# Router logits of chunks 0 to 7 on VectorE, with the rows of chunks 0 to 6 read back from DRAM

## The chip, the cores and the metric

One core of a Trainium2 chip runs the whole program. The metric is the device time of one execution in microseconds. A few words are used throughout: PE is TensorE's matrix multiply, PEld its weight load, DVE is VectorE, ACT is ScalarE, POOL is GpSimd, SP the engine that issues most DMAs. L1083 is line 1083 of the kernel before; the changed kernel has other line numbers, which are given where they matter.

## The reference

```python
def _attn_ref(q, k, v):                 # 4 batches, 8 heads, 576 positions, 64 dims
    ...
    return (out_up + out_local)         # pooled attention plus a band of +-3 positions
def _moe_ref(x, w_gate, w_val, w_out):  # x: 2304 tokens x 512
    g = x @ w_gate                      # 512 x 1536
    silu = g * (1.0 / (1.0 + np.exp(-g)))
    return silu * (x @ w_val) @ w_out   # 1536 x 512
def _moe2_ref(x, expert_emb, tau, w1, w2):
    xn = x / (np.linalg.norm(x, axis=-1, keepdims=True) + 1e-06)
    en = expert_emb / (np.linalg.norm(expert_emb, axis=-1, keepdims=True) + 1e-06)
    logits = xn @ en.T / tau            # 8 experts
    expert_idx = np.argmax(logits, axis=1)
    ...
    for e in range(E):                  # each token goes to one expert
        h = np.maximum(x[mask] @ w1[e], 0.0)
        out[mask] = gate_w[mask, None] * (h @ w2[e])
```

The three run one after another: attention, a gated layer, and a layer of eight experts of which each token uses one. The router needs, for each token, its norm and its eight logits.

## The kernel before, in words

The 2304 tokens are cut into nine chunks of 256 (`NCHUNK` is 9, `CT` is 256), numbered 0 to 8. A chunk's rows come in two blocks `m` of 128 tokens. Every fp32 product is made of three fast ones, with each operand split into a high and a low part.

For a chunk, `gemm1(c, p)` computes one of six blocks `p` of the hidden layer (L982); each has two **halves** `j`, of 24 matmuls, and one PSUM bank per half. `act_h` then works on a half: ACT tanh (L931), two DVE operations (L933, L935), an ACT cast (L938), and a subtraction on DVE or POOL (L940) that gives the low part. `gemm2(c, p)` multiplies that block by `w_out` (L1014) in four groups of three matmuls, and accumulates x2, the layer's output, in two PSUM banks. Chunks 0 and 1 run interleaved block by block; from chunk 2 on the order is one chunk after another. `gemm2` of a block comes one block later than its `gemm1`, and the last two blocks' second products stand together before the next chunk's first.

`x_split` and `x_piece` cut the attention's output of a chunk into high and low parts (L918 on ACT, L920 on DVE or POOL). There is one pair of buffers for it, so that a chunk's pieces are made after the last `gemm1` of the chunk before.

When x2 of a chunk is complete, `route(c)` is started. `route_m` copies each block of 128 rows to SBUF (L1051), has `store_x2` write it to the DRAM tensor `x2d` (L1205), and takes the sum of squares (L1054). Then the logits are made in one of two ways, by `ROWS_C`:

- Chunks 0 to 4 and 8: four transposes on PE (L1063), a copy to SBUF (L1068), and four matmuls with the normalised expert embeddings (L1073).
- Chunks 5 to 7: `route_rows`, eight DVE operations per block of rows (L1083). Each multiplies the 128x512 rows by one embedding, which lies on all partitions, and sums along the row. The embeddings are loaded for that by `prep_rows`, once attention has freed its buffers.

After that `route` scales the logits, takes the maximum and its index (L1127 to L1134), counts with two small matmuls on PE (L1143, L1144) at which place in its expert's list each token stands, and has POOL scatter the token numbers into the DRAM table `tab` (L1162, two indirect DMAs). Each chunk's `route` waits for the table entries of the chunk before, since `base`, the running count, goes from one to the next.

Expert 0's first two blocks of 128 places are filled from chunks 0 to 7 alone. `load_slots` reads the table, `load_slot` gathers the x2 rows by an indirect DMA on POOL (L1299), PE transposes them (L1309), ACT and DVE split them, and `expert(0)` begins (L1353) while chunk 8 is still being routed. `load_experts` and `split_w` load 64 pieces of expert weights and split them on ACT (L1238) and DVE (L1241).

The order on each engine is fixed at build time by a list scheduler, `Sched`: every operation has a cost in ns and a priority (a lower number goes first), and the scheduler walks through simulated time and gives each free engine the ready operation of the lowest number. `how=True` marks DVE operations that it doesn't let overlap with POOL's. On the chip each engine runs its list in order and waits by semaphores. Three lines of the part that the change touches:

```python
yield op("DVE", t_dve(DM) + 60, -0.3, True)                       # L1082, logits on DVE
yield op(("DVE", "POOL"), (t_dve(n), pool(n)), prio, True)        # both(): L920, L940
yield op("DVE", t_dve(CT), -0.5)                                  # L932, activation
```

Of the kernel before, what the change touches and what calls it, by code (L numbers as in the profile page):

```python
# [24 lines left out]
P = 128  # L25
B, H, S, D = 4, 8, 576, 64
HP = H // 2
DM = H * D
# [220 lines left out]
EARLY_N = range(NE)  # L249
ROWS_C = range(5, NCHUNK - 1)  # L250
NV = 4
# [6 lines left out]
def build(tc, a):  # L258
# [221 lines left out]

    en_rows = []

    def prep_rows():

        for n in range(B * HP):
            yield ("wait", ("done", n))
        sl = []
        for _ in range(5):
            sl.append((yield ("get", "aw")))
        for i in range(E // 2):  # L490
            yield dma(P * 4096)
            nc.sync.dma_start(out=sl[i], in_=bass.AP(tensor=end.tensor, offset=end.offset + 2 * i * DM, ap=[[0, P], [1, 2 * DM]]))
            en_rows.extend((sl[i][:, 0:DM], sl[i][:, DM:2 * DM]))
        en_rows.extend((sl[4][:, 0:DM], sl[4][:, DM:2 * DM]))
        sc.set("rows")

    def pget(n=1):
# [416 lines left out]
    def x_piece(c, k, xh, xl):  # L914
        yield ("wait", ("xr", c, k))
        src = x32[c][:, k, :]
        yield op("ACT", t_act(256), -1.0)
        nc.scalar.copy(xh[:, k, :], src)  # L918
        e = yield both(CT, -1.0)
        on[e].tensor_tensor(out=xl[:, k, :], in0=src, in1=xh[:, k, :], op=ALU.subtract)  # L920
        sc.set(("x", c, k))
# [71 lines left out]
    def gemm2(c, p):  # L993
# [3 lines left out]
        if p == NFB - 1:  # L997
            sc.spawn((c + 1) * 10 - 1, route(c))
        yield ("wait", ("w_out", p))
# [44 lines left out]
    def route_m(c, m, sv, lp):  # L1044
# [11 lines left out]
        if c in ROWS_C:  # L1056
            sc.put(x2cls(c), xp)
            sc.spawn(sc.cur.prio, route_rows(c, m, row, lp))
            return
# [5 lines left out]
        tcls = "w" if c == NCHUNK - 1 else "t2"  # L1065
        x2T = last_T[m] if last_T else (yield ("get", tcls))
        eng = yield psum(DM, hi)
# [10 lines left out]
    def route_rows(c, m, row, lp):  # L1078

        yield ("wait", "rows")  # L1080
        for e in range(E):
            yield op("DVE", t_dve(DM) + 60, -0.3, True)  # L1082
            nc.vector.scalar_tensor_tensor(out=en_rows[E + m], in0=row, scalar=1.0, in1=en_rows[e], op0=ALU.mult, op1=ALU.mult,  # L1083
                                           accum_out=lp[:, m, e:e + 1])
        sc.set(("rowT", c, m))
        sc.set(("lg", c, m))

    def route_norm(c, m, sv):
# [7 lines left out]
        sc.set(("norm", c, m))  # L1096

    last_T = []

    def route(c):  # L1100
        hi = -1.0
        if c == NCHUNK - 1:
            for m in range(2):
                last_T.append((yield ("get", "w")))
        if c > 0:
# [3 lines left out]
        lg, oh, t8, mx, mxi = lgt  # L1109
        sv = gm.tile([P, 4, 2], F32, tag="sv", name=f"sv{c}")  # L1110
        si = gm.tile([P, 2], I32, tag="si", name=f"si{c}")
        yield ("wait", ("x2", c, 0))
        if c in ROWS_C:
            lgs = lr = gm.tile([P, 2, E], F32, tag="lr", name=f"lr{c}")
        else:
            lp = lr = yield ("get", "ps")
            lgs = lp[:, 0:2 * E].rearrange("p (m e) -> p m e", m=2)
        for m in range(2):
            if c == NCHUNK - 1:
                sc.spawn(sc.cur.prio, route_m(c, m, sv, lr))  # L1120
            else:
                yield from route_m(c, m, sv, lr)
        for m in range(2):
# [105 lines left out]
    def stand_back():  # L1229

        if ("x2", NCHUNK - 1, 0) in sc.ev:
            yield ("wait", ("slot", NCHUNK - 1))
# [305 lines left out]
    with tc.manual_schedule():  # L1538
# [9 lines left out]
        sc.spawn(3, prep_en(), 0.0)  # L1548
        sc.spawn(3, prep_rows(), 0.0)
        for c in range(NCHUNK):  # L1550
            if c != 1:
# [126 lines left out]
```

## Time and profile before

| | |
|---|---|
| Runs | 867.78, 868.7, 866.0 us (median 867.78) |
| The profiled execution | 868.81 us, of which its span is 866.6 us |
| PE busy | 849.0 us, 98% of the span |
| DVE busy | 504.9 us, 58% |
| ACT busy | 377.1 us, 44% |
| POOL busy | 154.9 us, 18% |
| Mean granted clock of TensorE | 0.992 |

The profile is of one execution. Its span runs from the first to the last instruction that was recorded; 2.2 us of its own time lie outside. It can be read by stage: attention with the first chunks (to about 395 us), chunks 4 to 8 of the gated layer, the experts from 590 us, and the last scatters after 857 us.

### The profile page before, as it was taken

The page shows a single profiled execution, that of the slowest core. Times are in us where ns is not written, and L with a number is a line of the kernel's source. Part 1 is how long each engine was busy: PE and PEld are TensorE (multiplying, and loading weights), DVE is VectorE, ACT ScalarE, POOL GpSimd, SP SyncE. Part 2 cuts the span into 40 slices and gives each one's busy share as a digit, 9 for nine tenths or more (in the row PEclk, how much of TensorE's full clock was granted, in tenths as well). Part 3 has the DMA queues.
Part 4 walks back from the last instruction along what each step waited for, and adds up shares of the span by engine and source line. Part 5 has one row for each costly group of instructions (what it writes and reads, how often), then busy time and mean ns, then how long its engine had stood idle before and what let it go on. Part 6 is the DMA issues. An engine that isn't in the chain of part 4 may idle for free. (4 is left out here: it accounts for less than half of the span.)

```text
span 866.6 us, 17180 instructions
## 1 busy us (share of the span) xinstructions
PE 849.0 (98%) x6904; PEld 759.1 (88%) x6905; DVE 504.9 (58%) x1230; ACT 377.1 (44%) x906; POOL 154.9 (18%) x163
## 2 busy tenths in 40 slices
PE   9999999999999999999999999999999999999995
PEld 4788889999989989999999999999988888888884
DVE  4899999566555365673373654967464544545210
ACT  3878789444343243342221313345354444445120
POOL 4552300022102011010000000021310330331111
PEclk9999999999999999999999999999999999999998
DMA  8593445112121002122000000464565554453100
GB/s 255 191 327 119 137 155 178 54 37 83 57 82 58 1 26 58 57 83 98 2 25 1 25 1 26 123 194 122 153 206 177 169 182 148 161 186 120 30 27 28
DMA packets 53219, 90.21 MB, mean 104 GB/s; under 512 B 7878, under 2 KB 24646, under 8 KB 53136
## 3 DMA queue, kind: packets, MB, share of 16 engines
q1 hardware_dynamic: 48256, 78.83, 28.7%
q0 software_dynamic: 4160, 9.48, 3.3%
q8 instruction: 55, 0.90, 0.4%
q10 hardware_dynamic: 720, 0.77, 0.3%
q14 instruction: 28, 0.23, 0.1%
HBM read 80.05 MB, written 10.58 MB: 105 GB/s over the span
## 5 line engine op out<-in xcount | busy, mean ns | idle before, releaser
L982 PE MATMUL ps<-xhi,w 128*128 128x256 f32 x1504 | 294.0, 288 | 1.7 <-POOL w L428 1.3
L982 PEld LDWEIGHTS ps<-xhi,w 128*128 128x128 f32 x1504 | 242.5, 192 | 5.3 <-POOL w L428 1.5
L982 PE MATMUL ps<-xlo,w 128*128 128x256 f32 x752 | 213.3, 284 | 0.0
L982 PEld LDWEIGHTS ps<-xlo,w 128*128 128x128 f32 x752 | 144.7, 192 | 1.4
L1353 PE MATMUL ps<-xh,w 128*128 128x336 f32 (+1 forms) x512 | 124.3, 315 | 0.0
L1014 PE MATMUL x<-w,hh 128*128 128x512 f32 x384 | 120.9, 396 | 0.0
L933 DVE SCALAR_TENSOR_TENSOR th<-th,ps 128x256 f32<-128x256 f32 x108 | 45.1, 418 | 108.4 <-ACT th L931 106.0
L931 ACT ACTIVATE th<-ps 128x256 f32<-128x256 f32 x108 | 41.0, 380 | 128.5 <-PE ps L982 128.0
L1353 PEld LDWEIGHTS ps<-xh,w 128*128 128x128 f32 x512 | 88.3, 188 | 2.3
L1241 DVE TENSOR_TENSOR w<-w,w 128x1024 fp32r<-128x1024 f32 x64 | 76.9, 1217 | 21.8 <-ACT w L1238 20.9
L1353 PE MATMUL ps<-xl,w 128*128 128x336 f32 (+1 forms) x256 | 79.9, 312 | 0.0
L1014 PEld LDWEIGHTS x<-w,hh 128*128 128x128 f32 x384 | 68.3, 189 | 12.1 <-issue 0.4
L938 ACT CAST hh<-th 128x256 fp32r<-128x256 f32 x108 | 43.7, 405 | 79.9 <-DVE th L935 79.3
L1363 PE MATMUL x<-w,eh 128*128 128x512 f32 x248 | 78.3, 397 | 0.0
L1339 DVE SCALAR_TENSOR_TENSOR el<-ps,eh 128x336 fp32r<-128x336 f32 (+1 forms) x62 | 30.3, 493 | 80.6 <-ACT eh L1337 80.4
L1014 PE MATMUL x<-w,hl 128*128 128x512 f32 x192 | 74.9, 390 | 0.0
L1337 ACT ACTIVATE eh<-ps 128x336 fp32r<-128x336 f32 (+1 forms) x62 | 27.5, 443 | 90.7 <-PE ps L1353 84.6
L1238 ACT CAST w<-w 128x1024 fp32r<-128x1024 f32 x64 | 65.6, 1044 | 0.0
L1091 POOL TENSOR_TENSOR sv<-sv,half 128x1 f32<-128x1 f32 x18 | 10.4, 580 | 250.6 <-ACT x L1054 244.9
L1378 POOL DMA_INDIRECT out<-sg,tb x23 | 23.2, 1007 | 174.7 <-ACT sg L1370 166.1
L940 DVE TENSOR_TENSOR hl<-th,hh 128x256 fp32r<-128x256 f32 x94 | 39.8, 424 | 24.7 <-ACT hh L938 24.6
L1363 PEld LDWEIGHTS x<-w,eh 128*128 128x128 f32 x248 | 45.2, 188 | 9.0
(262 smaller groups left out, 1403.5 us busy)
## 6 DMA issues: line engine op xcount, KB each, us to landing
w<-w SPq DMA_DIRECT2D x64, 512.0 KB
w<-w_gate SPq DMA_DIRECT2D x10, 512.0 KB
w<-w_val SPq DMA_DIRECT2D x10, 512.0 KB
w<-w_out SPq DMA_DIRECT2D x10, 512.0 KB
w<-qk SPq DMA_DIRECT2D x16, 291.0 KB
aw<-qk SPq DMA_DIRECT2D x16, 291.0 KB
x2d<-sg SPq DMA_DIRECT2D x18, 256.0 KB
w<-vw SPq DMA_DIRECT2D x8, 320.0 KB
```

Of the source, the lines that this page charges most:

```text
L931: nc.scalar.activation(th, ps[:, 0:CT], AF.Tanh, scale=0.5)
L933: nc.vector.scalar_tensor_tensor(out=th, in0=th, scalar=1.0, in1=ps[:, 0:CT], op0=ALU.add, op1=ALU.mult)
L938: nc.scalar.copy(hh[:, j].bitcast(F32R), th)
L940: on[e].tensor_tensor(out=hl[:, j].bitcast(F32R), in0=th, in1=hh[:, j].bitcast(F32R), op=ALU.subtract)
L982: nc.tensor.matmul(ps[:, o:o + CT], ww[:, k, fs], xx[:, k, :], start=(k == 0 and n == 0), stop=(k == KD - 1 and n == 2))
L1014: nc.tensor.matmul(x2p[c, m], l[:, j, ms], r[:, js], start=(p == 0 and j == 0 and n == 0), stop=(p == NFB - 1 and j == 1 and n == 2))
L1238: nc.scalar.copy(hi.bitcast(F32R), raw)
L1241: nc.vector.tensor_tensor(out=lo.bitcast(F32R), in0=raw, in1=hi.bitcast(F32R), op=ALU.subtract)
L1337: nc.scalar.activation(hh[:, j, 0:n].bitcast(F32R), ps[:, 0:n], AF.Relu)
L1339: nc.vector.scalar_tensor_tensor(out=hl[:, j, 0:n].bitcast(F32R), in0=ps[:, 0:n], scalar=0.0, in1=hh[:, j, 0:n].bitcast(F32R), op0=ALU.max ...
L1353: nc.tensor.matmul(ps[:, 0:n], ww[:, k, fs], xx[:, k, 0:n], start=(k == 0 and t == 0), stop=(k == KD - 1 and t == 2))
L1363: nc.tensor.matmul(yt[:m], l, r, start=(first and n == 0), stop=(last and n == 2))
```

## The change

Logits of chunks 0 to 7 are all made on DVE. `ROWS_C` goes from chunks 5 to 7 to chunks 0 to 7, and the new `LATER` names chunks 0 to 6. For a chunk of `ROWS_C`, `gemm2` now starts `keep_rows`, which copies the rows, stores them to `x2d` and takes the norms; `route(c)` is started at the beginning of the program and waits for the norms and the logits. For a chunk of `LATER` the row buffer is free after the store, and `route_rows` waits until the embeddings are there (`rows`), takes one of three buffers `again` (half of an `aw` buffer and two halves of an `x32` buffer), reads the block of 128 rows back from `x2d` by a DMA on SP, and runs the eight multiplications. All of these write their product to the same scratch row `en_rows[E]`, where there were two, and their cost in the scheduler is 50 ns less.

Besides: pieces of x of chunks 3 to 8 go from priority -1.0 to -0.4, behind the activations' -0.5. `stand_back`, which holds the splits of expert weights back for the routing of chunk 8, does so from the last block of chunk 8 on. The two buffers for chunk 8's transposed rows are taken before the expert weights' (`last_slots`).

```diff
 EARLY_N = range(NE)
-ROWS_C = range(5, NCHUNK - 1)
+LATER = range(0, NCHUNK - 2)
+ROWS_C = range(0, NCHUNK - 1)
 NV = 4
...
-    en_rows = []
+    en_rows, again, svs, lrs = [], [], {}, {}
...
-        en_rows.extend((sl[4][:, 0:DM], sl[4][:, DM:2 * DM]))
+        en_rows.append(sl[4][:, 0:DM])
+        again.append(sl[4][:, DM:2 * DM])
+        sc.put("again", 0)
         sc.set("rows")
+        x = yield ("get", "x32")
+        x = x.rearrange("p k n -> p (k n)")
+        for i in range(2):
+            again.append(x[:, i * DM:(i + 1) * DM])
+            sc.put("again", i + 1)
...
     def x_piece(c, k, xh, xl):
         yield ("wait", ("xr", c, k))
         src = x32[c][:, k, :]
-        yield op("ACT", t_act(256), -1.0)
+        hi = -1.0 if c < 3 else -0.4
+        yield op("ACT", t_act(256), hi)
         nc.scalar.copy(xh[:, k, :], src)
-        e = yield both(CT, -1.0)
+        e = yield both(CT, hi)
         on[e].tensor_tensor(out=xl[:, k, :], in0=src, in1=xh[:, k, :], op=ALU.subtract)
...
         if p == NFB - 1:
-            sc.spawn((c + 1) * 10 - 1, route(c))
+            sc.spawn((c + 1) * 10 - 1, keep_rows(c) if c in ROWS_C else route(c))
...
         if c in ROWS_C:
             sc.put(x2cls(c), xp)
+            if c in LATER:
+                sc.set(("rowT", c, m))
             sc.spawn(sc.cur.prio, route_rows(c, m, row, lp))
             return
...
         sc.set(("rowT", c, m))
         tcls = "w" if c == NCHUNK - 1 else "t2"
-        x2T = last_T[m] if last_T else (yield ("get", tcls))
+        x2T = last_T[m] if c == NCHUNK - 1 else (yield ("get", "t2"))
         eng = yield psum(DM, hi)
         copy[eng](x2T[:, 0:DM], xp)
         sc.put(x2cls(c), xp)
...
         yield ("wait", "rows")
+        if c in LATER:
+            yield ("wait", ("x2d", c, m))
+            i = yield ("get", "again")
+            row = again[i]
+            yield dma(P * 2048)
+            t = 2 * c + m
+            nc.sync.dma_start(out=row, in_=x2d[t * P:(t + 1) * P, :])
         for e in range(E):
-            yield op("DVE", t_dve(DM) + 60, -0.3, True)
-            nc.vector.scalar_tensor_tensor(out=en_rows[E + m], in0=row, scalar=1.0, in1=en_rows[e], op0=ALU.mult, op1=ALU.mult,
+            yield op("DVE", t_dve(DM) + 10, -0.3, True)
+            nc.vector.scalar_tensor_tensor(out=en_rows[E], in0=row, scalar=1.0, in1=en_rows[e], op0=ALU.mult, op1=ALU.mult,
                                            accum_out=lp[:, m, e:e + 1])
-        sc.set(("rowT", c, m))
+        if c in LATER:
+            sc.put("again", i)
+        else:
+            sc.set(("rowT", c, m))
         sc.set(("lg", c, m))
...
+    def norms(c):
+        svs[c] = gm.tile([P, 4, 2], F32, tag=f"sv{c % 7}", name=f"sv{c}")
+        return svs[c]
+
+    def keep_rows(c):
+        sv = norms(c)
+        lrs[c] = gm.tile([P, 2, E], F32, tag=f"lr{c % 6}", name=f"lr{c}")
+        for m in range(2):
+            yield from route_m(c, m, sv, lrs[c])
+
     last_T = []
+
+    def last_slots():
+        yield ("wait", ("g1", NCHUNK - 2))
+        for m in range(2):
+            last_T.append((yield ("get", "w")))
...
     def route(c):
         hi = -1.0
-        if c == NCHUNK - 1:
+        if c in ROWS_C:
             for m in range(2):
-                last_T.append((yield ("get", "w")))
+                yield ("wait", ("norm", c, m))
+                yield ("wait", ("lg", c, m))
         if c > 0:
             yield ("wait", ("tab", c - 1))
         lgt = [gm.tile([P, 2, E], t, tag=nm, name=f"{nm}{c}") for nm, t in
                (("lg", F32), ("oh", F32R), ("t8", F32), ("mx", F32), ("mxi", U32))]
         lg, oh, t8, mx, mxi = lgt
-        sv = gm.tile([P, 4, 2], F32, tag="sv", name=f"sv{c}")
+        sv = svs[c] if c in ROWS_C else norms(c)
         si = gm.tile([P, 2], I32, tag="si", name=f"si{c}")
         yield ("wait", ("x2", c, 0))
         if c in ROWS_C:
-            lgs = lr = gm.tile([P, 2, E], F32, tag="lr", name=f"lr{c}")
+            lgs = lrs[c]
         else:
-            lp = lr = yield ("get", "ps")
+            lp = yield ("get", "ps")
             lgs = lp[:, 0:2 * E].rearrange("p (m e) -> p m e", m=2)
-        for m in range(2):
-            if c == NCHUNK - 1:
-                sc.spawn(sc.cur.prio, route_m(c, m, sv, lr))
-            else:
-                yield from route_m(c, m, sv, lr)
+            for m in range(2):
+                if c == NCHUNK - 1:
+                    sc.spawn(sc.cur.prio, route_m(c, m, sv, lp))
+                else:
+                    yield from route_m(c, m, sv, lp)
...
     def stand_back():
 
-        if ("x2", NCHUNK - 1, 0) in sc.ev:
+        if ("h", NCHUNK - 1, NFB - 1, 0) in sc.ev:
             yield ("wait", ("slot", NCHUNK - 1))
...
+        sc.spawn(NCHUNK * 10 + 3, last_slots(), 0.0)
+        for c in ROWS_C:
+            sc.spawn((c + 1) * 10 - 1, route(c), 0.0)
```

The built order shows what moves. First PE, in the second products (L1014, in the changed kernel L1023) around the routing of chunk 1, `x` being the x2 banks and `sg` the rows. Before:

```order
L1014 MATMUL x_1_112<-w_1_629,hl_1_99 128x512
L1063 MATMUL ps_1_106<-cn,sg_1_103 128x128 x4
L1014 MATMUL x_1_111<-w_1_629,hh_1_97 128x512
L1014 MATMUL x_1_111<-w_1_630,hh_1_97 128x512
L1014 MATMUL x_1_111<-w_1_629,hl_1_99 128x512
L1014 MATMUL x_1_112<-w_1_629,hh_1_97 128x512
L1014 MATMUL x_1_112<-w_1_630,hh_1_97 128x512
L1014 MATMUL x_1_112<-w_1_629,hl_1_99 128x512
L1073 MATMUL ps_1_108<-enT,sg_1_104 128x8 x4
L1014 MATMUL x_1_111<-w_1_629,hh_1_97 128x512
L1014 MATMUL x_1_111<-w_1_630,hh_1_97 128x512
L1014 MATMUL x_1_111<-w_1_629,hl_1_99 128x512
```

Now:

```order
L1023 MATMUL x_1_112<-w_1_629,hl_1_99 128x512
L862 MATMUL ps_1_108<-aw_3_2174 64x144 x4
L871 MATMUL ps_1_105<-aw_3_2175 64x58 x8
L871 MATMUL ps_1_105<-aw_2_2313,aw_3_2175 64x58 x8
L871 MATMUL ps_1_108<-aw_3_2175 64x58 x2
L871 MATMUL ps_1_108<-aw_3_2175 64x54 x2
L1023 MATMUL x_1_111<-w_1_629,hh_1_97 128x512
L1023 MATMUL x_1_111<-w_1_630,hh_1_97 128x512
L1023 MATMUL x_1_111<-w_1_629,hl_1_99 128x512
L1023 MATMUL x_1_112<-w_1_629,hh_1_97 128x512
L1023 MATMUL x_1_112<-w_1_630,hh_1_97 128x512
L1023 MATMUL x_1_112<-w_1_629,hl_1_99 128x512
```

The four transposes (L1063) and the four matmuls with the embeddings (L1073) are gone; part of an attention head (L862, L871) stands there instead, which had another place before.

Next DVE in the middle of chunk 6, three halves' activations (L933, L935, L940; in the changed kernel L942, L944, L949). Before:

```order
L933 SCALAR_TENSOR_TENSOR th_1_101<-th_1_101,ps_1_107 128x256
L935 SCALAR_TENSOR_TENSOR th_1_101<-th_1_101,ps_1_107 128x256
L940 TENSOR_TENSOR hl_1_100<-th_1_101,hh_1_98 128x256
L933 SCALAR_TENSOR_TENSOR th_1_102<-th_1_102,ps_1_110 128x256
L935 SCALAR_TENSOR_TENSOR th_1_102<-th_1_102,ps_1_110 128x256
L940 TENSOR_TENSOR hl_1_100<-th_1_102,hh_1_98 128x256
L933 SCALAR_TENSOR_TENSOR th_1_101<-th_1_101,ps_1_108 128x256
L935 SCALAR_TENSOR_TENSOR th_1_101<-th_1_101,ps_1_108 128x256
L940 TENSOR_TENSOR hl_1_99<-th_1_101,hh_1_97 128x256
```

Now, with `aw` and `x` the rows read back and `lr` the logits:

```order
L1188 TENSOR_TENSOR t_5224<-t_5224,oh_5223 128x16
L1216 RECIPROCAL cn<-gs_5275 128x2
L1101 SCALAR_TENSOR_TENSOR aw_10_4689,lr_3044<-x_3_4802,aw_11_4687 128x512
L1190 TENSOR_REDUCE sv_2334<-t_5224 128x2
L1101 SCALAR_TENSOR_TENSOR aw_10_4689,lr_3044<-x_3_4802,aw_11_4685 128x512
L1192 CAST si_5227<-sv_2334 128x2
L942 SCALAR_TENSOR_TENSOR th_1_102<-th_1_102,ps_1_107 128x256
L1222 TENSOR_TENSOR base<-base,ps_1_106 128x8
L944 SCALAR_TENSOR_TENSOR th_1_102<-th_1_102,ps_1_107 128x256
L1222 TENSOR_TENSOR base<-base,ps_1_106 128x8
L1101 SCALAR_TENSOR_TENSOR aw_10_4689,lr_3044<-x_3_4802,aw_10_4688 128x512
L949 TENSOR_TENSOR hl_1_100<-th_1_102,hh_1_98 128x256
```

Between the activations' operations there now stand the row multiplications (L1101) and the small operations of the routing of an earlier chunk. The half whose activation began just before these rows has its subtraction (L949) on POOL.

Last PE before the first product of expert 0, where `xs` are the gathered rows. Before, in the second product of block 3 of chunk 8:

```order
L1014 MATMUL x_1_112<-w_4_1652,hh_1_98 128x512
L1014 MATMUL x_1_112<-w_4_1666,hh_1_98 128x512
L1014 MATMUL x_1_112<-w_4_1652,hl_1_100 128x512
L1309 MATMUL ps_1_107<-cn,xs_1_6387 128x128 x4
L1309 MATMUL ps_1_109<-cn,xs_1_6388 128x128 x4
L1014 MATMUL x_1_111<-w_4_1652,hh_1_98 128x512
```

Now, in that of block 4:

```order
L1023 MATMUL x_1_112<-w_4_1915,hh_1_97 128x512
L1023 MATMUL x_1_112<-w_4_1916,hh_1_97 128x512
L1023 MATMUL x_1_112<-w_4_1915,hl_1_99 128x512
L1346 MATMUL ps_1_108<-cn,xs_1_6460 128x128 x4
L1023 MATMUL x_1_111<-w_4_1915,hh_1_97 128x512
L1023 MATMUL x_1_111<-w_4_1916,hh_1_97 128x512
L1023 MATMUL x_1_111<-w_4_1915,hl_1_99 128x512
L1346 MATMUL ps_1_106<-cn,xs_1_6461 128x128 x4
L1023 MATMUL x_1_112<-w_4_1915,hh_1_97 128x512
L1023 MATMUL x_1_112<-w_4_1916,hh_1_97 128x512
L1023 MATMUL x_1_112<-w_4_1915,hl_1_99 128x512
```

The transposes of expert 0's rows (L1309, now L1346) now stand apart, 21 and 18 second-product matmuls before the first product of expert 0; before, the last 3 of that block and all of the next stood behind them, 75 matmuls in all. On DVE the first operation of the routing of chunk 7 (L1127, now L1164) has moved from between the activations of halves 4 and 5 of chunk 8 to between those of halves 6 and 7. In the whole program PE has 40 transposes and 40 embedding matmuls fewer; DVE has 128 row multiplications instead of 48; POOL has 13 more of the activations' subtractions, 4 more of the x pieces' and 4 more operations of attention; SP has 14 more DMAs.

## Rows read from the trace of the kernel before

**Rows 1.** The page, part 1: busy us (share of the span) and instructions of each engine.
```profile
PE 849.0 (98%) x6904; PEld 759.1 (88%) x6905; DVE 504.9 (58%) x1230; ACT 377.1 (44%) x906; POOL 154.9 (18%) x163
```

**Rows 2.** Windows: stretch, us, each engine's busy us (instructions), PEclk, DMA share, GB/s.
```profile
175.00:385.00 210.00, 209.66 (x2061) 192.23 (x2059) 123.20 (x349) 81.38 (x261) 27.43 (x32) 1.00 0.17 55
385.00:435.00 50.00, 50.00 (x391) 46.86 (x391) 20.43 (x65) 13.20 (x38) 3.91 (x4) 1.00 0.13 43
435.00:554.00 119.00, 119.00 (x849) 112.49 (x848) 71.31 (x237) 32.95 (x85) 7.45 (x10) 1.00 0.07 23
554.00:590.00 36.00, 36.00 (x251) 33.58 (x250) 26.98 (x61) 17.83 (x31) 7.52 (x6) 1.00 0.61 184
590.00:850.00 260.00, 260.00 (x1487) 228.11 (x1486) 121.31 (x191) 106.20 (x170) 58.48 (x48) 1.00 0.44 137
```

**Rows 3.** Instructions of L1063 and L1073 on PE: min/median/max ns, first and last start.
```profile
L1063 PE MATMUL x<-cn,sg x40: 270/272/328, 175.5 to 593.8; 128*128 128x128 f32 x40
...
L1063 PE MATMUL ps<-cn,sg x8: 270/272/273, 197.8 to 202.9; 128*128 128x128 f32 x8
L1073 PE MATMUL ps<-enT,sg x80: 171/256/277, 177.3 to 385.3; 128*128 128x8 f32 x80
```

**Rows 4.** Timeline of PE, 197 to 202: start us, us, engine, line, operation.
```profile
197.78 0.60 PE L1063 MATMUL ps<-cn,sg 128*128 128x128 f32 x4
198.13 0.71 PE L1014 MATMUL x<-w,hh 128*128 128x512 f32 x2
...
198.91 0.62 PE L1014 MATMUL x<-w,hh 128*128 128x512 f32 x2
...
199.60 0.95 PE L1073 MATMUL ps<-enT,sg 128*128 128x8 f32 x8
200.41 0.71 PE L1014 MATMUL x<-w,hh 128*128 128x512 f32 x2
...
201.18 0.28 PE L982 MATMUL ps<-xhi,w 128*128 128x256 f32 x1
```

**Rows 5.** Timeline of DVE, 547 to 556 (same columns).
```profile
547.62 0.42 DVE L933 SCALAR_TENSOR_TENSOR th<-th,ps 128x256 f32<-128x256 f32 x1
...
550.50 0.42 DVE L933 SCALAR_TENSOR_TENSOR th<-th,ps 128x256 f32<-128x256 f32 x1
550.84 0.68 DVE L1083 SCALAR_TENSOR_TENSOR aw<-sg,aw 128x512 f32<-128x512 f32 x1
...
551.45 0.42 DVE L935 SCALAR_TENSOR_TENSOR th<-th,ps 128x256 f32<-128x256 f32 x1
551.78 0.68 DVE L1083 SCALAR_TENSOR_TENSOR aw<-sg,aw 128x512 f32<-128x512 f32 x1
...
552.73 0.69 DVE L1083 SCALAR_TENSOR_TENSOR aw<-sg,aw 128x512 f32<-128x512 f32 x1
...
553.46 0.69 DVE L1083 SCALAR_TENSOR_TENSOR aw<-sg,aw 128x512 f32<-128x512 f32 x1
...
554.19 0.17 DVE L1127 TENSOR_TENSOR lg<-lr,sv 128x16 f32<-128x16 f32 x1
554.28 1.22 DVE L1241 TENSOR_TENSOR w<-w,w 128x1024 fp32r<-128x1024 f32 x1
555.42 0.16 DVE L1130 MAX8 mx<-lg 128x8 f32<-128x8 f32 x1
```

**Rows 6.** Instructions of L940 on POOL.
```profile
L940 POOL TENSOR_TENSOR hl<-th,hh x14: 726/736/2234, 92.1 to 578.0; 128x256 fp32r<-128x256 f32 x14
```

**Rows 7.** Timeline of POOL, 569 to 573; last, idle time before and who ended it.
```profile
569.11 2.23 POOL L940 TENSOR_TENSOR hl<-th,hh 128x256 fp32r<-128x256 f32 x1 [3.62 <-ACT hh L938]
571.49 1.05 POOL L1299 DMA_INDIRECT xs<-x2d,tb  x1
```

**Rows 8.** Timeline of PE, 577 to 591.
```profile
577.61 1.03 PE L1309 MATMUL ps<-cn,xs 128*128 128x128 f32 x8
...
590.39 0.28 PE L1353 MATMUL ps<-xh,w 128*128 128x256 f32 x1
```

## The prediction

> **What bounds the kernel now.** I read the views from the whole to the part. The page gives PE as busy for 98% of the span, DVE for 58% [rows 1]. PE's busy time alone doesn't show a bound, since its instructions overlap, so I took the stretches next: from 175 us to 590 us PE lacks 0.34 us in all, and in 590 to 850 nothing [rows 2]. In those stretches anything that leaves PE's list shortens the span, unless PE then has to wait for something else. [...] DVE there has 71.31 us of work in 119 us between 435 and 554, the stretch of chunks 6 and 7 and parts of their neighbours [rows 2]: room, but not for everything. So the question has two sides: how much PE time goes, and whether DVE, with 80 more row multiplications, still delivers in time.
>
> **What goes from PE.** For chunks 0 to 4 there were 40 transposes: 32 of the 40 that write an x2 bank (the other 8 are chunk 8's, which stay) and 8 for chunk 1, whose x2 lies in `ps` banks. The 80 matmuls with the embeddings that the trace counts for rows in `sg` all go [rows 3]; each of the program's 40 is two in the trace. Their listed durations overlap, so I take start to start. A group of three second-product matmuls alone takes 198.91 to 199.60, 0.69 us. With four transposes ahead of it a group takes 197.78 to 198.91, 1.13 us: 0.44 us for the transposes. With eight embedding matmuls ahead, 199.60 to 201.18, 1.58 us: 0.89 us for them [rows 4]. There are ten such blocks of rows: 10 x (0.44 + 0.89) = **13.3 us** less on PE. ACT and DVE also lose ten copies of transposed rows, which cost nothing either way: PE doesn't lack anything there that they make.
>
> **What comes to DVE.** 80 row multiplications more, and those of chunks 0 to 4 wait until attention is done, so 128 of them, with eight chunks' routing, lie between the end of chunk 5 and the middle of chunk 8. A row multiplication takes 0.61 us when another kind of operation follows (550.84 to 551.45), but 0.73 us when the next is also one (552.73 to 553.46). An activation operation takes 0.33 us (551.45 to 551.78), a small routing operation about 0.1 us (554.19 to 554.28), a weight split 1.14 us (554.28 to 555.42). A half of the first product takes PE 2.88 us (547.62 to 550.50) [rows 5]; a chunk is 12 of these and 24 groups of 0.69 us [rows 4], 51.1 us. By the built order of the changed kernel:
>
> - Chunk 6: 48 row multiplications, 15 of them directly ahead of another: 33 x 0.61 + 15 x 0.73 = 31.1 us; 34 operations of 256 columns, 11.2 us; 55 small ones, 5.5 us. Together 47.8 of 51.1 us.
> - Chunk 7: 44 (9 ahead of another), 27.9 us; 11.2 us; 5.8 us for 58 small ones: 44.9 of 51.1 us.
> - Chunk 8 up to the routing of chunk 7: 18 (1 ahead of another), 11.1 us; 16 of 256 columns, 5.3 us; two weight splits, 2.3 us; 21 small ones, 2.1 us: 20.8 us of about 22.8 us.
>
> So DVE fits, at 88 to 94%. But PE meets DVE at fixed places in its list: eight pairs of counting matmuls (L1143) must wait for the one-hot rows, and in a list this full the DVE operation they need stands behind a row multiplication about whenever PE arrives. I charge half of one, 0.3 us, for each of the eight: **2.4 us**. The ends are 0 (what is queued in front of PE's wait is always done in time) and the 5.5 us more of the first rival below; I take 2.4 because the sums leave DVE free time in each chunk. There is no gain below 0: DVE gets nothing faster that PE waits for.
>
> **What else moves.** The 14 reads of rows go through SP; DMA is busy 7% between 435 and 554 [rows 2], and a gather of a block of rows has landed at the latest 577.61 - 571.49 = 6.1 us after POOL began to issue it [rows 7, 8]. DVE needs a block every 51.1 / 6 = 8.5 us and there are three buffers, so I cost the reads at nothing; behind them on SP stand only stores of x2 and, in chunk 8, the expert weights. If that cover goes, DVE stands still with the activations behind it (second rival). The x pieces behind the activations have the eight groups of second products that end a chunk, 8 x 0.69 = 5.5 us; they need some 2 us more than before at most: nothing. Weight buffers for chunk 8 taken earlier delay the first expert weights by about two halves (5.8 to 8.6 us); eight of the splits still stand ahead of expert 0's first product, where it needs the first of them: nothing. If that is wrong PE waits at the first product of expert 0. The one scratch row instead of two is in the 0.73 us already.
>
> **The sum.** The profiled execution took 868.81 us, 2.2 us of it outside the span, and 1.0 us more than the median of the runs shown, 867.78 us. 868.81 - 13.3 + 2.4 = 857.9 us for it, and by the same difference on the median **856.9 us**.
>
> **Rivals.**
>
> 1. DVE and POOL shut each other out. POOL's subtraction takes 0.736 us in the median of 14, but one of them 2.234 us [rows 6], the one at 569.11 [rows 7], so something can hold POOL up threefold. From the end of chunk 5 to the routing of chunk 7 the new order gives POOL 15 operations of 256 columns where before it had none; if DVE stood still for each, that is 15 x 0.73 = 11.0 us. About half of it falls into DVE's free time (3.3, 6.2 and 2.0 us by the sums above), so PE loses 5.5 us more: 862.4 us. For it speaks that single long row; against it that 14 rows have a median as short as that. [...]
> 2. The read-back comes too late, and the kernel gets slower. Past 8.5 us from the release of a buffer to the landing, DVE stands still in each of 14 reads. At 10.5 us that is 28 us, of which DVE's free 11.5 us take up part: PE loses 16.5 us, and 856.9 + 16.5 = 873.4 us. It turns the sign from about 9.9 us on, (10.9 + 11.5) / 14 = 1.6 us past 8.5. Against it stand the 6.1 us above, which were an upper bound beside a DMA share of 0.61 [rows 2].
> 3. Expert 0's rows arrive late. Before, the routing of chunk 7 began on DVE at 554.19 [rows 5], the gather was issued at 571.49 [rows 7], PE transposed at 577.61 and began expert 0 at 590.39 [rows 8]. The new order begins that routing two halves later (2.88 and 2.88 + 4 x 0.69, together 8.5 us) and has the transposes 5.6 instead of 12.8 us ahead of expert 0, 7.2 us later. That leaves 22.1 us where there were 23.4. PE didn't wait before, so at most 1.3 us are missing; if DVE is also 3 us late there, five row multiplications, PE waits 4.3 us: 861.2 us.
> 4. The change doesn't do what it says: PE has the work off its list but waits as long elsewhere, and the time stays at 867.8 us. Attention, whose work on DVE and ACT it can't shorten, could be what sets PE's pace. Against it: 209.66 us busy in 210 [rows 2], where a PE that waits for attention would show gaps.
>
> **How the numbers follow.** My forecast has a chance of 0.63; rival 1 0.15; rival 2 0.04; rival 3 0.13; rival 4 0.05. About 0.3%, 2.6 us, can be told from no change. The forecast and rivals 1 and 3 are all faster by more than that; of rival 1 I take 0.03 off, for a lock that leaves nothing of the gain (11.0 instead of 5.5 us) or more: faster 0.88, the same 0.07, slower 0.05. For the range: with no loss at all 867.8 - 13.3 = 854.5 us, less the 1.8 us by which the lowest of the three runs lies under their median, 852.7 us; upward it takes in rivals 3 and 1, to 862.5 us. Rivals 2 and 4, and the worse part of rival 1, are left out.
>
> **What the profile of the changed kernel would show.** Right: no transposes or embedding matmuls for chunks 0 to 4; PE still without gaps from 175 us on; the first product of expert 0 at about 579.5 us instead of 590.39; DVE busy over 85% of chunks 6 and 7, with row multiplications of 0.61 to 0.73 us. Wrong: idle time of PE at the counting matmuls, at the transposes of expert 0's rows or at second products (ended by a subtraction on POOL, rival 1); DVE idle for a DMA ahead of a row multiplication (rival 2); gaps on PE between 175 and 385 us (rival 4). Expert 0's stages from there to the end should keep their length; if they are longer, the late weight buffers cost something after all.

## The result and the profile after

The changed kernel takes 857.03 us in the median of 4 runs (855.71 to 858.38), the kernel before 868.24 us in 4 runs on the same chip: ratio 0.9875, 95% interval 0.9851 to 0.9900. The forecast was 856.9 us. The number came out, but not by its own sum: a loss that it charged didn't come, and one that it left out did.

The profiled execution took 858.38 us, its span is 856.5 us. Part 1 of its page (engine: busy us, share of the span, instructions):

```profile
PE 835.1 (97%) x6784; PEld 745.2 (87%) x6785; DVE 544.6 (64%) x1368; ACT 371.3 (43%) x897; POOL 170.5 (20%) x184
```

Against [rows 1] PE has 120 instructions and 13.9 us less, DVE 39.7 us more. The windows of the changed kernel, cut a little earlier than those of [rows 2] because everything comes earlier (columns as there):

```profile
175.00:385.00 210.00, 210.00 (x2058) 192.38 (x2057) 118.80 (x282) 79.90 (x261) 24.62 (x32) 1.00 0.17 55
385.00:420.00 35.00, 35.00 (x270) 32.55 (x269) 19.18 (x54) 8.30 (x22) 0.74 (x1) 1.00 0.25 84
420.00:545.00 125.00, 124.84 (x896) 117.93 (x895) 118.00 (x455) 33.11 (x92) 30.47 (x34) 1.00 0.18 46
545.00:580.00 35.00, 31.84 (x214) 28.86 (x213) 25.27 (x61) 16.18 (x28) 7.99 (x7) 1.00 0.57 176
580.00:850.00 270.00, 266.59 (x1514) 232.41 (x1512) 121.98 (x190) 109.79 (x174) 60.53 (x50) 1.00 0.44 136
```

Read the second and third figure of each row. Between 420 and 545 us DVE is busy for 118.00 of 125 us, 94%, and PE still lacks only 0.16 us. The loss is in the next row, where PE lacks 3.16 us in 35, at the handover from the last chunk to the experts; before it lacked nothing there. (The last row holds the end of the program.) All waits of PE between 175 and 860 us: what waited, for whom, us in total, times, longest.

```profile
PE ps L1346 <- issue: 1.6, 1, 1.6
PE ps L1346 <- DMA xs<-x2d,tb: 1.6, 1, 1.6
PE ps L1180 <- DVE oh L1171: 0.2, 1, 0.2
```

L1346 are the transposes of the gathered rows, L1180 is the first counting matmul of a routing. On the timeline of PE (start, us, and at the end the idle time ahead):

```profile
570.34 0.39 PE L1023 MATMUL x<-w,hl 128*128 128x512 f32 x1
572.33 0.63 PE L1346 MATMUL ps<-cn,xs 128*128 128x128 f32 x4 [1.60 <-issue]
...
575.21 0.66 PE L1346 MATMUL ps<-cn,xs 128*128 128x128 f32 x4 [1.56 <-DMA xs<-x2d,tb]
...
579.80 0.28 PE L1390 MATMUL ps<-xh,w 128*128 128x256 f32 x1
```

For the two gathers, which POOL begins at 564.82 and 568.25, the view of `xs` gives the time to the landing (least, median, most):

```profile
DMA to landing us min/median/max: 6.9/7.2/7.4
```

The rows of the first gather landed at 572.24, after 7.42 us, those of the second at 575.17, after 6.92 us, so both waits, also the one put down to "issue", are for rows. How far the change is ahead at the first activation operations of two chunks shows what PE saved before that. Where chunk 2 and chunk 8 begin on DVE before:

```profile
185.48 0.42 DVE L933 SCALAR_TENSOR_TENSOR th<-th,ps 128x256 f32<-128x256 f32 x1 [0.17 <-ACT th L931]
...
541.86 0.42 DVE L933 SCALAR_TENSOR_TENSOR th<-th,ps 128x256 f32<-128x256 f32 x1 [1.12 <-ACT th L931]
```

After, these two rows read

```profile
183.11 0.41 DVE L942 SCALAR_TENSOR_TENSOR th<-th,ps 128x256 f32<-128x256 f32 x1
...
527.53 0.41 DVE L942 SCALAR_TENSOR_TENSOR th<-th,ps 128x256 f32<-128x256 f32 x1
```

The lead is 2.4 us, then 14.3 us, at expert 0's first product 590.39 - 579.80 = 10.6 us [rows 8], and at the end of the span 866.6 - 856.5 = 10.1 us. So the handover gives back 3.7 us, 3.2 of them in those two waits. The experiments ask why.

### The profile page after: what moved, and what is told of

Its sections match the earlier page's. It is cut to its first block, busy times and chain, and to the rows that moved or that the text cites. A ratio compares the mean times of both kernels' runs of the same rounds, so it can differ in the third digit from the quotient of the medians.

```text
span 856.5 us, 17156 instructions
## 1 busy us (share of the span) xinstructions
PE 835.1 (97%) x6784; PEld 745.2 (87%) x6785; DVE 544.6 (64%) x1368; ACT 371.3 (43%) x897; POOL 170.5 (20%) x184
## 5 line engine op out<-in xcount | busy, mean ns | idle before, releaser
L991 PE MATMUL ps<-xhi,w 128*128 128x256 f32 x1504 | 290.0, 287 | 1.4 <-POOL w L429 1.3
L1023 PE MATMUL x<-w,hh 128*128 128x512 f32 x384 | 121.2, 397 | 0.0
L940 ACT ACTIVATE th<-ps 128x256 f32<-128x256 f32 x108 | 41.0, 381 | 127.3 <-PE ps L991 126.7
L1278 DVE TENSOR_TENSOR w<-w,w 128x1024 fp32r<-128x1024 f32 x64 | 76.5, 1216 | 22.1 <-ACT w L1275 22.1
L942 DVE SCALAR_TENSOR_TENSOR th<-th,ps 128x256 f32<-128x256 f32 x108 | 44.8, 416 | 69.9 <-ACT th L940 69.7
L1023 PEld LDWEIGHTS x<-w,hh 128*128 128x128 f32 x384 | 68.1, 189 | 12.1 <-issue 0.6
L1023 PE MATMUL x<-w,hl 128*128 128x512 f32 x192 | 74.9, 390 | 0.0
L949 POOL TENSOR_TENSOR hl<-th,hh 128x256 fp32r<-128x256 f32 x27 | 20.2, 747 | 161.6 <-ACT hh L947 150.9
L1101 DVE SCALAR_TENSOR_TENSOR aw<-x,aw 128x512 f32<-128x512 f32 x72 | 49.9, 693 | 1.0
```

The source lines that it names most:

```text
L940: nc.scalar.activation(th, ps[:, 0:CT], AF.Tanh, scale=0.5)
L942: nc.vector.scalar_tensor_tensor(out=th, in0=th, scalar=1.0, in1=ps[:, 0:CT], op0=ALU.add, op1=ALU.mult)
L991: nc.tensor.matmul(ps[:, o:o + CT], ww[:, k, fs], xx[:, k, :], start=(k == 0 and n == 0), stop=(k == KD - 1 and n == 2))
L1023: nc.tensor.matmul(x2p[c, m], l[:, j, ms], r[:, js], start=(p == 0 and j == 0 and n == 0), stop=(p == NFB - 1 and j == 1 and n == 2))
L1101: nc.vector.scalar_tensor_tensor(out=en_rows[E], in0=row, scalar=1.0, in1=en_rows[e], op0=ALU.mult, op1=ALU.mult, accum_out=lp[:, m, e:e + 1])
L1278: nc.vector.tensor_tensor(out=lo.bitcast(F32R), in0=raw, in1=hi.bitcast(F32R), op=ALU.subtract)
```

## The experiments

Each edit is against the changed kernel unless it says otherwise; all times are medians, and each ratio is to the kernel before on the same chip.

**1. The priorities alone**, in the kernel before: do the reordered activations and the later weight splits do anything without the removed PE work? (Chunk 8's weight buffers are taken as early as in the change, too.)

```diff
-        yield op("ACT", t_act(256), -1.0)
+        hi = -1.0 if c < 3 else -0.4
+        yield op("ACT", t_act(256), hi)
...
-        if ("x2", NCHUNK - 1, 0) in sc.ev:
+        if ("h", NCHUNK - 1, NFB - 1, 0) in sc.ev:
```

> The kernel before with the side edits alone: pieces of x behind the activations, weight splits standing back earlier, the two weight buffers for chunk 8 taken earlier; the logits of chunks 0 to 4 stay on PE. Theory (the gain is PE's time for transposes and embedding matmuls): the same as before, 868 us within 2.6 us. Rival (the new priorities bring part of the gain): at least 3 us faster.

Measured: 869.09 us, ratio 1.0005 (0.9988 to 1.0023). Nothing, as expected: by the interval these bring at most 1 us of the gain in the kernel before.

**2. Only chunks 2 to 7 on DVE**: four of the ten blocks go back to PE.

```diff
-LATER = range(0, NCHUNK - 2)
-ROWS_C = range(0, NCHUNK - 1)
+LATER = range(2, NCHUNK - 2)
+ROWS_C = range(2, NCHUNK - 1)
```

> The changed kernel with chunks 0 and 1 back on PE, so that chunks 2 to 7 are on VectorE and 96 row multiplications instead of 128 stand in the late stretch. Theory: four blocks of rows cost PE 4 x 1.4 = 5.6 us again; VectorE is relieved by some 21 us, so the wait at the transposes of expert 0's rows (3.2 us in the changed kernel) may shrink or go: 859.4 to 862.6 us. Rival (VectorE's load in chunks 5 to 8 is what costs time, PE's work is cheap): no slower than the changed kernel, 857 us or less.

Measured: 868.29 us, ratio 0.9996 (0.9967 to 1.0024): a miss by 6 us. At chunk 8 it starts at 534.49, still 7.4 us ahead of before; then it loses all of that. Its waits of PE from 385 us on, and two of its windows:

```profile
PE ps L1346 <- issue: 3.2, 1, 3.2
PE ps L1346 <- DMA xs<-x2d,tb: 1.5, 2, 1.0
PE ps L1180 <- DVE oh L1171: 1.0, 1, 1.0
```

```profile
567.00:570.50 3.50, 0.26 (x4) 0.09 (x2) 0.00 (x0) 0.28 (x1) 1.55 (x2) 1.00 0.89 286
570.50:575.00 4.50, 4.02 (x20) 3.63 (x21) 2.11 (x4) 2.02 (x4) 0.00 (x0) 0.68 0.17 66
```

The order built for this kernel has the same transposes 72 and 69 matmuls earlier on PE, counted from the first product of expert 0. PE reaches the first of them 32.8 us into chunk 8 instead of 43.2, but the gather begins only 8.3 us earlier in the chunk (29.0 us into it instead of 37.3; on POOL at 563.49, for 3.02 us). So it loses at the same place, and there the granted clock falls to 0.68 after PE has stood for 3.2 us. The four blocks themselves cost what they should: 14.3 - 7.4 = 6.9 us less lead at chunk 8, 1.0 of them the wait at L1180, 1.5 us a block.

**3. Expert 1's weights planned later**: is it the load traffic that delays the gathered rows?

```diff
         for e in range(E):
+            if e == 1:
+                for j in range(2):
+                    yield ("wait", ("gather", 0, j))
             for nm, dst in (("w1", w1s), ("w2", w2s)):
```

> The changed kernel, with the weight loads of expert 1 started only after the two gathers of expert 0's rows are issued. Theory (the gathers land late, 7.4 and 6.9 us after issue, because four weight loads of 512 KB are issued at the same time): they land some 4.5 us after issue, both waits of 1.6 us at the transposes go, 853.5 to 854.5 us. Rival (the routing of chunk 7 is late because VectorE is full, the loads don't matter): the waits stay, 857 us. A third way: the waits go, but expert 1's weights come late and PE waits in expert 1.

Measured: 859.09 us, ratio 0.9890 (0.9866 to 0.9913): a miss, no better than the change. PE still waits 1.23 and 0.81 us at the first transposes and 1.1 us more at those for the next rows. The first gather is as slow as ever, which the timeline of POOL shows:

```profile
564.24 3.59 POOL L1339 DMA_INDIRECT xs<-x2d,tb  x1 [6.33 <-DVE hl L949]
568.14 1.01 POOL L1339 DMA_INDIRECT xs<-x2d,tb  x1 [0.30 <-DVE th L942]
```

But the edit didn't move the loads on the chip. It holds them back in the order that is planned; the four of expert 1 that lie around the gathers stand on SP as before, first in the changed kernel, then here:

```profile
562.58 6.42 SPq L1292 DMA_DIRECT2D w<-w  x4
```

```profile
562.05 6.83 SPq L1295 DMA_DIRECT2D w<-w  x4
```

The first of them still starts 2.2 us ahead of the first gather. So this run says nothing for or against the load traffic.

**4. More time between gather and transposes.** The order is fixed ahead of the run; it places the transposes by an allowance for the landing.

```diff
-        yield ("lag", 5500 if e == 0 and j < 2 else 2800 if e < 2 else 9500)
+        yield ("lag", 8500 if e == 0 and j < 2 else 2800 if e < 2 else 9500)
```

> The changed kernel, with 3 us more in the scheduler for the landing of expert 0's gathers: on PE the two groups of transposes stand 12 matmuls (2.7 us) later in the second product, nothing else is meant to move. Theory: the rows land at the same time, so that PE waits less at the transposes (under 1 us in all), but the splits of the rows then end later against the first product of expert 0; half of the 3.2 us is won at best: 855 to 857 us. Rival (the waits come from something that stands ahead of the transposes on PE's list): no change in the waits.

Measured: 854.32 us, ratio 0.9834 (0.9807 to 0.9861). That is a little better than expected. One wait of 0.90 us is left, at the second transposes. So the loss was PE standing ahead of rows that weren't there, while it had other work that could go first.

**5. Why the rows are late: the weight splits held back.** In the changed kernel the first gather and the operations of DVE beside it read (POOL, then DVE; [rows 7] had 1.05 us for such a gather):

```profile
564.82 3.12 POOL L1336 DMA_INDIRECT xs<-x2d,tb  x1 [6.80 <-DVE xs L1332]
568.25 1.01 POOL L1336 DMA_INDIRECT xs<-x2d,tb  x1 [0.30 <-DVE th L942]
```

```profile
564.74 2.29 DVE L1278 TENSOR_TENSOR w<-w,w 128x1024 fp32r<-128x1024 f32 x2
567.66 0.42 DVE L942 SCALAR_TENSOR_TENSOR th<-th,ps 128x256 f32<-128x256 f32 x1 [0.64 <-ACT th L940]
568.60 1.22 DVE L1278 TENSOR_TENSOR w<-w,w 128x1024 fp32r<-128x1024 f32 x1 [0.51 <-ACT w L1275]
```

Two weight splits, each with two inputs in SBUF, end at 567.03; the gather ends 0.91 us later, at 567.94, about the time that it takes by itself. Runs 2, 3, 4, 8, 10 and 11 show the same 0.92 us from the end of the second split to the end of the first gather. (Not every overlap holds a gather: the split at 568.60 begins 0.35 us into the second gather, which takes its usual 1.01 us, while the first gathers of runs 3, 10 and 11 are held by splits that begin about 0.4 us into them. Why is open.) The edit lets no split start on DVE between the routing of chunk 7 and 4 us behind the issue of both gathers:

```diff
+        if ("slot", NCHUNK - 2) in sc.ev:
+            yield ("wait", ("pair", 0))
         yield op("DVE", t_dve(1024), None, True)
```

> Theory (expert 0's rows come late because the first gather is slow on POOL beside the two-input weight splits of VectorE, 3.12 us after the change against 1.05 before): with the splits held back until both gathers are issued, the first gather takes about 1.05 us on POOL, its rows land about 2 us earlier, TensorE's waits at the first transposes of gathered rows shrink from 3.2 us to 1 us or less, and the time is 854 to 855.5 us. Rival (the landing itself is late, whatever POOL does): the gather is short or not, but the rows still land 7 us behind it, the waits stay near 3 us and the time is 857 us. If the splits come too late for expert 0, a wait at its first products takes the gain back.

Measured: 855.66 us, ratio 0.9866 (0.9846 to 0.9886); the changed kernel in the same comparison, as run 8, 858.61 us, ratio 0.9908 (0.9890 to 0.9926).

> The changed kernel again, beside the three others on the same chip: 857 us, with TensorE waiting about 3.2 us at the first transposes of expert 0's gathered rows and nowhere else over 0.3 us.

The gathers of run 5:

```profile
565.50 1.04 POOL L1338 DMA_INDIRECT xs<-x2d,tb  x1 [7.08 <-DVE xs L1334]
566.85 1.01 POOL L1338 DMA_INDIRECT xs<-x2d,tb  x1 [0.31 <-issue]
```

Here 1.04 us, in run 8 2.70 us. In run 5 the rows land 5.2 and 5.85 us after the first gather began (570.69, 571.35), in run 8 6.6 and 9.2 us (571.27, 573.93), and PE doesn't wait at the first transposes at all, where run 8 waits 1.18 and 1.29 us, in all less than the 3.2 us expected of it. Two waits for later rows, 0.73 and 0.87 us, are new in run 5.

So the splits are the cause of the slow first gather, and of its late rows: from its end on POOL to the landing it is 3.9 us in run 8 and 4.1 us in run 5. For the second rows, which end the second wait, they explain about half. These land 3.4 us later in run 8 (9.2 less 5.85). The first gather's longer time on POOL delays the second gather by 1.65 us of that. The rest comes behind its issue: it takes POOL 1.01 us in both runs, but lands 6.2 us after its start in run 8 and 4.5 us in run 5 (first run 8, then run 5; the least figure of each row is the second gather's):

```profile
DMA to landing us min/median/max: 6.2/6.4/6.6
```

```profile
DMA to landing us min/median/max: 4.5/4.8/5.2
```

Holding the splits also moved the weight loads. Run 8 issues two at 566.50 and 568.07, around its second gather at 567.70; run 5 issues none between 564.81 and 569.01, around its own at 566.85. Whether the loads made the second landing slow is not shown: run 3, which was meant to test it, left them where they were.

**6. Both edits**, 4 and 5 together.

> Longer landing allowance for expert 0's rows (as in the run before) and the splits held back as well: by the theory the 0.9 us that was left at the second transposes goes too, so no TensorE wait over 0.3 us at the transposes of gathered rows, and 853 to 854.3 us. Rival (the allowance alone did all that can be done): 854.3 us, as with the allowance alone.

Measured: 856.66 us, ratio 0.9882 (0.9861 to 0.9904), not better than either. The transposes are now later than the rows need, and PE waits behind them:

```profile
PE ps L1397 <- DVE xl L1355: 0.8, 1, 0.8
```

That is a miss of both ends of the expectation. The rest of the distance to run 4 I can't name.

**7. The lock of rival 1, DVE and POOL shutting each other out, unplanned.** The program that builds the order keeps POOL's and DVE's operations with two SBUF inputs apart; here that rule is taken out, on top of edit 4.

```diff
-        if eng == "DVE" and k.how and self.free["POOL"] > t:
-            t = self.free["POOL"] + 1
-        elif eng == "POOL":
-            t = max(t, self.port)
```

> The order is planned without the rule that keeps VectorE's work and POOL's work with two SBUF inputs apart (with the longer allowance). If the lock of the two engines is what the prediction's first rival priced, row multiplications of 0.7 us turn into 1.1 us or more where POOL's halves run beside them, TensorE waits at the counting matmuls and the logits of chunks 5 to 8, and the time is 3 to 8 us above the run with the allowance alone (857 to 862 us). If the lock costs TensorE nothing even unplanned, 854.3 us within 1 us.

Measured: 878.17 us, ratio 1.0119 (1.0097 to 1.0141), worse than both ends of the expectation. POOL's subtractions, first in the changed kernel, then here (min/median/max ns), and PE's waits here from 385 to 545 us:

```profile
L949 POOL TENSOR_TENSOR hl<-th,hh x27: 722/739/822, 92.0 to 572.1; 128x256 fp32r<-128x256 f32 x27
```

```profile
L945 POOL TENSOR_TENSOR hl<-th,hh x36: 721/748/1309, 66.2 to 584.5; 128x256 fp32r<-128x256 f32 x36
```

```profile
PE ps L1176 <- DVE oh L1167: 3.9, 5, 1.6
PE x L1019 <- POOL hl L945: 1.5, 2, 1.2
PE x L1019 <- ACT hh L943: 0.3, 1, 0.3
```

5.7 us of waits in chunks 5 to 8, where the change has 0.16. But the rule acts everywhere, and this order is another one from the start: chunk 2 begins on DVE at 195.91 instead of 183.11, so most of the loss isn't in the part that was to be tested. And of the longest wait, 1.61 us, only some 0.4 us is the lengthened row multiplication in front of it (1.09 us instead of 0.69); the rest is where the order puts things. So this run shows longer single operations, subtractions on POOL up to 1.31 us where the change has 0.82 at most and a row multiplication of 1.09 us beside one of them (444.57 to 445.38), and that this order, planned without the rule, took 878.17 us; it gives no clean price for chunks 5 to 8.

**9 to 11. A version meant to be faster than both.** Splits held as in 5, with a slightly longer allowance, and beside it edit 4 and the changed kernel once more.

```diff
-        yield ("lag", 5500 if e == 0 and j < 2 else 2800 if e < 2 else 9500)
+        yield ("lag", 6000 if e == 0 and j < 2 else 4000 if e < 2 else 11000)
```

> Splits held back until the first gathers are issued, and a landing allowance longer by 0.5 us for expert 0's rows, by 1.2 us for the other rows of experts 0 and 1, by 1.5 us for later ones. By the theory (what was left of TensorE's waits in the run with the splits held alone, 0.73 and 0.87 us, is rows placed too close behind their gathers) no TensorE wait over 0.5 us behind the first 175 us, and 853.5 to 855 us. Rival (later rows push the first subtraction of their low halves back, and TensorE waits there instead, as in the run with both edits): 855.5 to 857 us.

> The allowance of 8.5 us alone, once more, beside the changed kernel on the same chip: faster than the changed kernel by 2 to 3 us (one wait of about 0.9 us left at the second transposes instead of two of 1.2 to 1.6 us).

> The changed kernel beside the two others: 857 to 858.6 us, TensorE waiting 2.5 to 3.2 us at the first transposes of expert 0's gathered rows.

Measured: 853.95 us (853.80 to 855.48, 5 runs), ratio 0.9847 (0.9826 to 0.9867); edit 4 alone 854.46 us (854.19 to 855.36, 5 runs), 0.9847 (0.9827 to 0.9867); the changed kernel 857.23 us (855.32 to 859.79, 4 runs), 0.9870 (0.9843 to 0.9896). The intervals of the first and the last just overlap, so that the 3.3 us between them rest on the traces beside the medians. Run 10 has no wait of PE over 0.15 us left; run 11 waits 1.19 and 1.02 us at the first transposes, less than expected. All that PE of the first of them waits for between 175 and 860 us:

```profile
PE ps L1180 <- DVE oh L1171: 0.2, 1, 0.2
```

From the start of chunk 8 on DVE to expert 0's first product it takes 48.69 us (526.64 to 575.33), the kernel before 48.53 us, the changed kernel 52.27 us. So what the handover lost is won back. That edit 4 alone does as well says that there are two cures: don't be early, or make the rows come sooner.

## Why the prediction came out

**What goes from PE, 13.3 us: right in kind, a little small.** From the start of chunk 2 to that of chunk 8 the kernel before takes 356.38 us, the changed one 344.42 us: 11.96 us, and eight of the ten blocks lie in between, 1.5 us each instead of 1.33. Part of the difference are the gaps that PE had ahead of these very operations, 0.34 us between 175 and 385 us [rows 2] and 0.00 after; the remaining microsecond I haven't split up. Run 2 gives 1.5 us a block too. That is 14.3 us of lead at chunk 8.

**DVE fits at 88 to 94%: right, a little low.** It is 94% between 420 and 545 us. By chunks, from one first activation to the next, it is 49.5 of 52.0 us in chunk 6 and 47.7 of 50.5 in chunk 7, where the sums had 47.8 and 44.9; up to the routing of chunk 7 it is 19.9 of 21.3 us in chunk 8, for 20.8 of 22.8. So chunk 7 was fuller than predicted. Row multiplications follow each other at 0.73 us in the median of 38 pairs, and are followed by something else after 0.61 us in 90, the two prices taken from [rows 5].

**2.4 us for counting matmuls that wait: wrong.** The step "in a list this full the DVE operation they need stands behind a row multiplication about whenever PE arrives" failed. One of nine pairs waited, 0.16 us. The fifth routing is an example of why the others didn't: DVE begins it at 496.79 and PE counts at 500.31, 3.5 us later, with other matmuls up to its start. A full engine isn't a late one: the order gives PE work until the one-hot rows are there. The lower end of that term, 0, was nearly the value.

**Rival 3, expert 0's rows late: it happened.** Its place was right, and it weighed 0.13 where it should have stood in the sum, at 3.2 us. Its price, 4.3 us with "DVE also 3 us late", named the wrong cause. DVE began the routing of chunk 7 at 548.83, 21.3 us into chunk 8 instead of 12.3, about the 8.5 us of the sum. From there to the landing it took 23.4 us for the first rows and 26.3 us for the second (572.24 and 575.17), where the prediction had 22.1 us to spend. With the splits held, in run 5, it takes 21.4 and 22.0 us (549.33 to 570.69 and 571.35): the 22.1 us would have done. What broke them was POOL, held for 2.1 us in the first gather by DVE's splits (3.12 us there, 1.04 us in run 5). The second rows then took 2.4 us longer from the start of their own gather than in run 5 (6.92 and 4.50 us); the cause of that is open.

**Rival 1, the lock: it shows in single operations, but was planned around.** Beside the long subtraction that it started from, on POOL from 569.11 to 571.34 [rows 7], DVE made no row multiplication but a weight split:

```profile
569.59 1.16 DVE L1241 TENSOR_TENSOR w<-w,w 128x1024 fp32r<-128x1024 f32 x1
```

The subtraction took 2.23 us, against 0.74 in the median [rows 6], and ended 0.59 us after the split. So the kernel before had a sign that a split can hold POOL up, just ahead of the gather. In the changed kernel 1 of 128 row multiplications is long (1.10 us, at 449.04, where the median is 0.69), and so are five tiny operations (0.51 to 0.72 us). At all six places a subtraction on POOL begins 0.10 to 0.23 us before a row multiplication ends, and the long operation follows on DVE. One such place, on DVE and on POOL:

```profile
484.19 0.70 DVE L1208 TENSOR_TENSOR lg<-lg,mx 128x16 f32<-128x16 f32 x1
```

```profile
484.10 0.76 POOL L949 TENSOR_TENSOR hl<-th,hh 128x256 fp32r<-128x256 f32 x1 [4.96 <-ACT hh L947]
```

L1208 takes 0.17 us in the median of nine. The prediction charged 15 halves against DVE; there were 12 between 400 and 550 us, and PE lost nothing by them. That DVE stands still for the whole 0.73 us of each was the author's estimate; the six long operations took 0.34 to 0.55 us more than their medians. What did cost PE time was the gather, which the rival didn't look at: beside two weight splits, subtractions with two SBUF inputs, it took 2.70 us in run 8, without them 1.04 us in run 5. No run here shows what in the gather was held up.

**Read-backs at nothing (rival 2): right.** The landings of the 14 reads, from the instructions of L1098:

```profile
DMA to landing us min/median/max: 2.6/3.4/7.0
```

All are under the 8.5 us that a block has, and no row multiplication waited for one. (The turning point of 9.9 us in that rival is a slip: 8.5 + 1.6 is 10.1.) **Rival 4** is excluded by the 210.00 us busy in 210. **The x pieces and later weight buffers** cost nothing that a wait shows; run 1 shows the priorities to be neutral in the kernel before, within about 2 us.

**The sum** was 13.3 - 2.4 = 10.9 us. What happened by chunk 8 and the handover is 14.3 - 3.7 = 10.6 us. Saving too small by 1.0, a loss of 2.4 that wasn't there, a loss of 3.7 that was left out: 1.0 + 2.4 - 3.7 = -0.3 us. That expert 0 begins at 579.80, where 579.5 was said, and that the time is within 0.2 us of the forecast, is in part luck: these three errors cancel.

## What to carry to other kernels

When a stage gets shorter, look at the fixed allowances that stood behind its length: here the 5.5 us that the order allows for a gather were enough before, and too few once the gather met two weight splits and landed late, and that became nearly the only wait. Don't charge a wait because the engine that delivers is full; look where the order puts the delivery and the need. And look at what VectorE does while GpSimd issues an indirect DMA that something is waiting for: here the gather took GpSimd 2.70 us beside two weight splits (run 8) and 1.04 us with the splits held back (run 5).

## What the runs showed of the hardware

The granted clock fell after a short stand of PE in runs 2 and 11, and in other executions it didn't. In the changed kernel, with waits of 1.60 and 1.56 us, it stays at 1.00 in the windows from 565 to 590 us, as it does in run 8 with 1.18 and 1.29 us; when the same kernel ran again as run 11, with 1.19 and 1.02 us, these were its windows:

```profile
573.00:575.00 2.00, 1.20 (x7) 0.72 (x6) 1.41 (x3) 0.00 (x0) 0.73 (x1) 1.00 0.58 207
575.00:577.00 2.00, 1.78 (x7) 1.59 (x8) 0.52 (x2) 0.82 (x2) 0.00 (x0) 0.62 0.00 0
577.00:579.00 2.00, 2.00 (x6) 1.53 (x6) 1.62 (x2) 0.71 (x1) 0.00 (x0) 0.53 0.00 0
```

At 0.53 a group of three second-product matmuls starts 1.28 us after the last (577.22 to 578.50), where it is 0.69 us at a granted clock of 1.00 [rows 2, 4]. So shorter waits than in the profile above ended up dearer, from 52.27 to 52.94 us for the handover. What decides it is open.
